# Moving the first feed-forward weight splits to other tiles and other engines at the seam between attention and the first dense layer

## The chip, the core and the metric

The kernel runs on one core of one Trainium2 chip. The metric is the device time of one execution in microseconds (us), as a median over runs. The core has TensorE (PE, with its weight loads shown apart as PEld), VectorE (DVE), ScalarE (ACT), GpSimd (POOL) and SyncE (SP), which here only issues transfers.

## The reference

Three stages follow each other. The first is an attention with pooled queries, the second a dense feed-forward layer, the third a mixture of four dense experts.

```python
q_pool = q.reshape(B, H, S // 2, 2, D).mean(axis=3)          # B 2, H 8, S 1152, D 64
scores = (1 / sqrt(D)) * q_pool @ k.transpose(0, 1, 3, 2)
attn = exp(scores - scores.max(-1)); attn /= attn.sum(-1) + 1e-9
x = (attn @ v) -> rows of 1152 tokens x 512
h = x @ w_in                                                 # 512 -> 2048
x = maximum(0.01 * h, h) @ w_out                             # 2048 -> 512
out = sum_e p[:, e] * (maximum(x @ w1[e], 0) @ w2[e])        # 4 experts, 512 -> 1024 -> 512
```

## The kernel before

Every product is made of three TensorE products: each operand is held as a high half and a low half (`h` and `l`, the rounded value and the rest), and high by high, high by low and low by high are added in PSUM.

**Attention.** It runs over 8 pairs of heads with 9 tiles of 128 query rows each, 72 tiles in all (`tiles`, numbered i; t is the tile within its pair). For a tile, TensorE makes the scores (`emit_s`, line 355), VectorE scales them out of PSUM and takes the row's extreme (line 358), ScalarE makes the exponentials (line 364), VectorE the reciprocal of the sum (line 372), and `emit_norm` multiplies the tile by it (line 374, GpSimd, but VectorE for the last two tiles). TensorE then transposes the tile in three groups of three (line 395) through three PSUM banks, ScalarE copies each group to `th` (line 399) and VectorE makes `tl`, the low half (line 101). The scores run three tiles ahead of the transposes and use the same three PSUM banks each time, so the next scores wait for line 358. The second products (line 422, from `queue_av`) sit in a list, and `run_av` takes a few of them per tile; at the end of each of four column blocks, ScalarE and VectorE write `xf`, `xh` and `xl` (lines 430, 431, 94, 101). These are the layer's input.

**The first dense layer.** It has 16 blocks f of 128 hidden columns. Its weights come as 64-bit numbers whose two 32-bit words need six steps, `split64`, to become two halves of a float: s0 on ScalarE (line 113), s1 and s2 on VectorE (lines 116, 120; with `fast=0` ScalarE's line 122 too), s3 on VectorE, ScalarE and an engine `e` (lines 127, 128, 130), s4 (line 134 on VectorE, or line 136 on GpSimd with `fast=0`), and s5 on `e` (line 139). `e` is VectorE with `fast=2`, and GpSimd otherwise. `prep_a` does this for the input weights (tiles `a`, raw words `wa`), `prep_b` for the output weights (`b`, `wb`). There are three `a` tiles and two raw buffers of each kind; `load_a` and `load_b` issue the next transfer on SP.

For each block TensorE runs 36 products (`first_layer`, lines 190 to 192). The product on line 192 reads the low half of `a`, which the last step, line 139, completes. Then `evac_leaky` has ScalarE take the block out of PSUM (line 589, a leaky relu), write `gh`, and VectorE write `gl`. The first products of block 0 are spread over the last four attention tiles (`f0`). From block 3 on, some 18 or 36 products of the second matrix (`second_moe1`, lines 610 to 612) follow each block.

**What sets the order.** The whole order is written out by hand: the program's order is the queue of each engine, and an engine stops at an instruction whose operands are not ready. `ahead` holds the weight steps that are put between attention tiles; `AT0` says at which tile of the last pair the splits of blocks 0 and 1 begin. Block 2's split (`next_a(2, 2)`) comes after the attention, and so do those of the output weights.

Of the kernel before, what the change touches and what calls it, by code (L numbers as in the profile page):

```python
# [16 lines left out]
ALU = mybir.AluOpType  # L17
# [21 lines left out]
def tile_kernel(ctx: ExitStack, tc: tile.TileContext, q, k, v, w_in, w_out, probs, w1, w2, out):  # L39
# [125 lines left out]
    def prep_a(f, tmp, fast=0):  # L165
        h, l = (a_b[f % 3][:, i] for i in range(2))
        a_t[f] = tuple(t.rearrange("p (a b) -> p a b", a=KD) for t in (h, l))
        return split64(h, l, wa_raw[f % 2].rearrange("p (a b) -> p a b", b=2), tmp, fast)

    def prep_b(f, tmp):  # L170
        h, l = b_t[f] = tuple(b_b[f % 8][:, i] for i in range(2))
        return split64(h, l, wb_raw[f % 2].rearrange("p (a b) -> p a b", b=2), tmp, 1)


    turn = [0]
# [20 lines left out]
    with ExitStack() as actx:  # L196
# [133 lines left out]

        L2 = 6

        AT0 = (0, 6)

        F0N = (0, 2, 2, 2)
        s_sb, chunks = {}, {}
# [33 lines left out]
        def emit_norm(i):  # L370
            e, st = s_sb[i]
            DVE.reciprocal(st[:, 3:4], st[:, 2:3])  # L372
            eng = POOL if i < len(tiles) - 2 else DVE
            eng.tensor_scalar(e, e, st[:, 3:4], 1.0, op0=ALU.mult, op1=ALU.mult)  # L374

        def chunk(n, name):
            if (n, name) not in chunks:
# [72 lines left out]
        with tc.manual_schedule():  # L450
# [52 lines left out]

            def begin(f):
                def go():
                    ahead_a[f] = prep_a(f, tmp)
                return go

            def step(f, i):
                return lambda: ahead_a[f][i] and ahead_a[f][i]()  # L510

            for f, t0 in enumerate(AT0):
                ahead.setdefault(t0, []).extend([begin(f), step(f, 0)])
                for d, ks in enumerate([(1, 2), (3,), (4,), (5,)]):
                    ahead.setdefault(t0 + 1 + d, []).extend([step(f, k_) for k_ in ks])

            for t, load in [(4, load_b), (4, load_b), (AT0[0] + 5, load_a), (AT0[1] + 5, load_a)]:
                ahead.setdefault(t, []).append(load)


# [2 lines left out]
            for i, (n, t) in enumerate(tiles):  # L523
                if i in begin_at:
                    for d, fs in enumerate(prep_pair(begin_at[i])):
                        steps.setdefault(i + d, []).extend(fs)
                lead = 2 if i < L2 else 3

                upto("s", emit_s, i + lead - (i == L2))
                if i == 0:  # L530

                    upto("norm", emit_norm, i + lead - 1)
                upto("sum", emit_sum, i + lead - 1 - (i == L2))
                emit_t(i, lambda: upto("norm", emit_norm, i + lead - 1 - (i == L2)))
                run_av(AVB.get(t, AVD) if i > L2 else AV0.get(t, AVD))
                if i == L2:
                    upto("exp", emit_exp, i + lead - 1)
                    upto("s", emit_s, i + lead)
                    upto("sum", emit_sum, i + lead - 1)
                    upto("norm", emit_norm, i + lead - 1)  # L540
                    run_av(AVD)
                if i == len(tiles) - 4:

                    f0_ps, mms = first_layer(0, xh, xl)
                    f0 = [(k_, c) for k_ in range(KD - 1) for c in range(NC)] + [(KD - 1, c) for c in range(NC)]
                if i >= len(tiles) - 4:
                    for _ in range(F0N[t - 5]):
                        mms(*f0.pop(0))
                upto("exp", emit_exp, i + lead)
                if t in (1, 4, 6, 8):  # L550
                    name, w = {1: ("A1", 256), 4: ("A2", 320), 6: ("B1", 320), 8: ("B2", 256)}[t]
                    queue_av(n, name, w, fast=n == len(pairs) - 1 and t > 4)
                for f in steps.get(i, []):
                    f()
                if n == len(pairs) - 1:
                    for f in ahead.get(t, []):
                        f()
            run_av(1e9)
            for t in range(9, 16):
                for f in ahead.get(t, []):  # L560
                    f()
            while f0:
                mms(*f0.pop(0))

# [7 lines left out]
    def tmp():  # L572
        return next(ring)

    def next_b(f):
        return prep_b(f, tmp) + [load_b]

    def view(t, n=NC):
        return t.rearrange("p (c w) -> p c w", c=n)
# [190 lines left out]

    with tc.manual_schedule():
        SP.dma_start(pr, probs)
        run(next_a(2, 2))
        run(evac_leaky(0, f0_ps), next_a(3), next_b(0))
        ps, mms = first_layer(1, xh, xl)
        for k_ in range(KD):
            for c in range(NC):
                mms(k_, c)
        run(evac_leaky(1, ps), next_b(1))

        when_b = {f: [f - 1] for f in range(3, 15)} | {15: [14, 15]}

# [1 line left out]
        for f in range(2, n1):  # L784
            ps, mms = first_layer(f, xh, xl)
            for k_ in range(KD):
                for c in range(NC):
                    mms(k_, c)
            if f == n1 - 1:
                for b in when_b[f]:  # L790
                    run(next_b(b))
                run(evac_leaky(f, ps))
            else:
                run(evac_leaky(f, ps), next_a(f + 2, f == 2), *[next_b(b) for b in when_b.get(f, [])])
            if f == n1 - 2:
                load_w1(0)
            if f >= GROUPS[second[0][0]][-1] + 2:
                second_moe1(*second.pop(0))
# [88 lines left out]
```

## Time and profile before

| | us |
|---|---|
| median of 3 runs (843.22 to 845.43) | 844.21 |
| the profiled execution | 844.05 |
| its span, from first to last instruction | 842.0 |
| PE busy | 820.8 (97%) |
| VectorE busy | 574.1 (68%) |
| ScalarE busy | 434.5 (52%) |
| GpSimd busy | 417.3 (50%) |

The span is 2.05 us shorter than the execution's time. The attention's last scores end at about 244 us of the span and its last second products at about 261 us; the first dense layer begins at 250.5 us, among the last tiles. The granted clock of TensorE over the span is 0.996 of its full 2.4 GHz.

### The profile page before, as it was taken

The numbers are of one execution on the slowest core, as the hardware profiler recorded it, in microseconds if no ns is written. First come the engines' busy times: TensorE is split into PE (matmuls) and PEld (weight loads), VectorE is DVE, ScalarE is ACT, GpSimd is POOL, SyncE is SP. The second block draws the span as 40 slices with busy tenths as digits, with TensorE's granted clock in tenths as the row PEclk, the third lists the DMA queues.
The fourth block names the chain that finished last, engine by engine and source line by source line (L and its number), as shares of the span: only waits on it lengthen the run. The fifth ranks groups of instructions, "written<-read, shape, count | busy, mean of one in ns | idle before, by whom it ended". The sixth has DMA issues, their size and how long they took to land.

```text
span 842.0 us, 13590 instructions
## 1 busy us (share of the span) xinstructions
PE 820.8 (97%) x5091; PEld 775.6 (92%) x5091; DVE 574.1 (68%) x947; ACT 434.5 (52%) x764; POOL 417.3 (50%) x366
## 2 busy tenths in 40 slices
PE   6899999999989899999999999999999999999998
PEld 5799999999989799999999998989898998989897
DVE  5889999999998979767765762736445363625332
ACT  5889999999976555433432641505142341506030
POOL 3788888888753678556561240506042331504020
PEclk9999999999999999999999999999999999999999
DMA  7347644563401233331130120302011110201012
GB/s 224 90 132 189 181 105 136 162 174 96 138 26 52 100 100 101 100 99 52 51 101 26 51 76 1 100 1 88 13 51 51 50 52 4 98 0 52 0 38 100
DMA packets 25713, 68.65 MB, mean 82 GB/s; under 512 B 2992, under 2 KB 7856, under 8 KB 25648
## 3 DMA queue, kind: packets, MB, share of 16 engines
q1 hardware_dynamic: 25424, 67.43, 26.8%
q8 instruction: 40, 0.66, 0.3%
q10 hardware_dynamic: 224, 0.36, 0.1%
q14 instruction: 25, 0.20, 0.1%
HBM read 48.91 MB, written 2.36 MB: 61 GB/s over the span
## 4 chain that ended last, share of the span: by engine, by line
PE 89%; DVE 7%; issue 2%; ACT 1%; POOL 1%; DMA 1%; SPq 0%; DVEq 0%; POOLq 0%; ACTq 0%
PE ps L713 21%; PE ps L355 9%; PE ps L758 8%; PE ps L760 8%; PE ps L759 8%; PE ps L422 7%; PE ps L395 7%; PE ps L612 4%; PE ps L610 4%; PE ps L611 4%; PE ps L192 3%; PE ps L191 3%; PE ps L190 3%; DVE e L358 2%; DVE tl L101 1%
## 5 line engine op out<-in xcount | busy, mean ns | idle before, releaser
L101 POOL TENSOR_TENSOR bb<-w2r,bb 128x512 fp32r<-128x512 f32 x32 | 40.8, 1297 | 259.0 <-ACT bb L94 259.0
L767 DVE SCALAR_TENSOR_TENSOR oacc<-ps,pw,oacc 128x512 f32<-128x512 f32 (+1 forms) x64 | 47.5, 742 | 100.4 <-PE ps L760 100.4
L101 DVE TENSOR_TENSOR tl<-ps,th 128x384 fp32r<-128x384 f32 (+1 forms) x240 | 112.2, 505 | 3.2 <-ACT th L399 2.8
L758 PE MATMUL ps<-bb,gg 128*128 128x512 f32 (+1 forms) x292 | 112.9, 387 | 0.0
L760 PE MATMUL ps<-bb,gg 128*128 128x512 f32 (+1 forms) x292 | 112.8, 386 | 0.0
L759 PE MATMUL ps<-bb,gg 128*128 128x512 f32 (+1 forms) x292 | 112.8, 386 | 0.0
L713 PE MATMUL ps<-yT,ws 128*128 128x288 f32 x768 | 111.3, 296 | 0.0
L374 POOL TENSOR_SCALAR e<-e,st 128x1152 f32<-128x1152 f32 x70 | 86.3, 1234 | 42.8 <-DVE st L372 25.2
L713 PEld LDWEIGHTS ps<-yT,ws 128*128 128x128 f32 x768 | 105.6, 188 | 0.9 <-ACT cb L730 0.3
L358 DVE TENSOR_SCALAR_CACHE_REDUCE e<-ps 128x1152 f32<-128x1152 f32 x72 | 97.5, 1355 | 11.0 <-PE ps L355 9.7
L355 PE MATMUL ps<-k,qst 128*128 128x384 f32 x438 | 94.4, 346 | 7.9 <-DVE e L358 3.8
L399 ACT CAST th<-ps 128x384 fp32r<-128x384 f32 (+1 forms) x240 | 91.4, 459 | 17.9 <-PE ps L395 16.3
L719 ACT COPY ca<-ps 128x576 f32<-128x576 f32 x16 | 10.3, 641 | 167.1 <-PE ps L713 155.3
L364 ACT ACTIVATE e<-e,st 128x1152 f32<-128x1152 f32 x72 | 91.3, 1268 | 4.8 <-DVE e L358 2.8
L395 PE MATMUL ps<-ident,e 128*128 128x128 f32 x648 | 83.9, 275 | 5.1 <-POOL e L374 3.4
L355 PEld LDWEIGHTS ps<-k,qst 128*128 128x128 f32 x438 | 75.6, 190 | 13.0 <-DVE e L358 6.9
L713 PE MATMUL ps<-yB,ws 128*128 128x288 f32 x576 | 84.4, 296 | 0.0
L395 PEld LDWEIGHTS ps<-ident,e 128*128 128x128 f32 x648 | 75.1, 141 | 9.7 <-POOL e L374 5.1
L713 PEld LDWEIGHTS ps<-yB,ws 128*128 128x128 f32 x576 | 79.6, 188 | 0.6
L192 PE MATMUL ps<-xh,a 128*128 128x384 f32 x192 | 65.1, 339 | 2.8 <-POOL a L139 2.8
L190 PE MATMUL ps<-xh,a 128*128 128x384 f32 x192 | 64.8, 338 | 0.7 <-ACT gf L589 0.7
L760 PEld LDWEIGHTS ps<-bb,gg 128*128 128x128 f32 x292 | 54.9, 188 | 11.4 <-DVE gg L739 0.2
(126 smaller groups left out, 1724.9 us busy)
## 6 DMA issues: line engine op xcount, KB each, us to landing
wa<-in_w_in SPq DMA_DIRECT2D x16, 512.0 KB, 3.4
wb<-in_w_out SPq DMA_DIRECT2D x16, 512.0 KB, 4.3
wf<-in_w SPq DMA_DIRECT2D x32, 256.0 KB, 2.8
w2r<-in_w SPq DMA_DIRECT2D x16, 512.0 KB, 3.4
qst<-rq SPq DMA_DIRECT2D x28, 288.0 KB, 4.6
rv<-in_v SPq DMA_DIRECT2D x8, 576.0 KB, 6.6
rk<-in_k SPq DMA_DIRECT2D x7, 576.0 KB, 6.0
rq<-in_q SPq DMA_DIRECT2D x7, 576.0 KB, 5.3
```

The source lines that it names most:

```text
L101: eng.tensor_tensor(dst, src, f32(high), op=ALU.subtract)
L190: PE.matmul(ps[:, c, :CW], wh[:, k_], src_h[:, k_, cs], start=k_ == 0, stop=False)
L192: PE.matmul(ps[:, c, :CW], wl[:, k_], src_h[:, k_, cs], start=False, stop=k_ == KD - 1)
L355: PE.matmul(ps[:, c, :CW], x, y, start=m == 0, stop=m == len(mms) - 1)
L358: DVE.tensor_scalar(e, ps[:, :, :CW], -0.5 / float(D) ** 0.5, None, op0=ALU.mult, op1=ALU.min, accum_out=st[:, 0:1])
L364: ACT.activation(e, e, AF.Exp, bias=st[:, 0:1], scale=-1.0, accum_out=st[:, 1:2])
L395: PE.transpose(ps[:, j], e[:, (3 * g + j) * 128:(3 * g + j + 1) * 128], ident)
L399: ACT.copy(h, ps[:, :, s0:s0 + w])
L713: PE.matmul(ps[:, c, :HW], w[wi][:, i, ks], y[:, yi, k, c * HW:(c + 1) * HW], start=bool(first and k == 0 and m == 0), stop=k == 1 and m = ...
L758: PE.matmul(ps, gh[:, ts_], wh, start=f == fs[0], stop=False)
L759: PE.matmul(ps, gh[:, ts_], wl, start=False, stop=False)
L760: PE.matmul(ps, gl[:, ts_], wh, start=False, stop=f == fs[-1])
```

## The change

- The split of block 0's input weights starts three tiles earlier: s0 and s1 go to tiles of the pair before, s2 to tile 0, and s3 to s5 stay where they were. `AT0` now gives a tile of the last pair for every step (-3 is the third tile before it).
- Block 1's split gets `fast=2`: what GpSimd and ScalarE's line 122 did in it is VectorE's.
- Block 2's split moves from behind the attention to its last tiles and among the last second products, also with `fast=2`. The list of second products, before emptied in one go, is now emptied block by block between the steps.
- Block 3's and 4's input weights and the first two blocks of output weights get `fast=2`.
- The last two tiles are normalised by GpSimd, not VectorE.
- A one-element leaky relu on ScalarE stands after the last exponential, so that the table load which stood ahead of the first `evac_leaky` stands there.

```diff
-    def prep_b(f, tmp):
+    def prep_b(f, tmp, fast):
...
-        AT0 = (0, 6)
+        AT0 = ((-3, -2, 0, 2, 3, 4), (6, 7, 7, 8, 9, 9), (8, 10, 10, 11, 11, 11))
...
-            eng = POOL if i < len(tiles) - 2 else DVE
-            eng.tensor_scalar(e, e, st[:, 3:4], 1.0, op0=ALU.mult, op1=ALU.mult)
+            POOL.tensor_scalar(e, e, st[:, 3:4], 1.0, op0=ALU.mult, op1=ALU.mult)
...
-                    ahead_a[f] = prep_a(f, tmp)
+                    ahead_a[f] = prep_a(f, tmp, 2 if f else 0)
...
-            for f, t0 in enumerate(AT0):
-                ahead.setdefault(t0, []).extend([begin(f), step(f, 0)])
-                for d, ks in enumerate([(1, 2), (3,), (4,), (5,)]):
-                    ahead.setdefault(t0 + 1 + d, []).extend([step(f, k_) for k_ in ks])
-
-            for t, load in [(4, load_b), (4, load_b), (AT0[0] + 5, load_a), (AT0[1] + 5, load_a)]:
+            for f, ts in enumerate(AT0):
+                ahead.setdefault(ts[0], []).append(begin(f))
+                for k_, t in enumerate(ts):
+                    ahead.setdefault(t, []).append(step(f, k_))
+
+            for t, load in [(4, load_b), (4, load_b), (5, load_a), (9, load_a), (12, load_a)]:
...
-                if n == len(pairs) - 1:
-                    for f in ahead.get(t, []):
-                        f()
-            run_av(1e9)
-            for t in range(9, 16):
+                for f in ahead.get(i + 9 - len(tiles), []):
+                    f()
+                if i == len(tiles) - 3:
+
+                    ACT.activation(warm, warm, AF.Lrelu, alpha=0.01)
+
+            for t in range(9, 13):
                 for f in ahead.get(t, []):
                     f()
+                while t < 11 and av:
+                    cost, f = av.pop(0)
+                    f()
+                    if not cost:
+                        break
+            assert not av
...
-        run(next_a(2, 2))
-        run(evac_leaky(0, f0_ps), next_a(3), next_b(0))
+        run(evac_leaky(0, f0_ps), next_a(3, 2), next_b(0, 2))
...
-        run(evac_leaky(1, ps), next_b(1))
+        run(evac_leaky(1, ps), next_b(1, 2))
...
-                run(evac_leaky(f, ps), next_a(f + 2, f == 2), *[next_b(b) for b in when_b.get(f, [])])
+                run(evac_leaky(f, ps), next_a(f + 2, 2 * (f == 2)), *[next_b(b) for b in when_b.get(f, [])])
```

TensorE's own instructions stand in the same order in both kernels. What moves stands on the other engines, at three places. In the rows below a name's number is that of its buffer: `ct_118` and `c_120`, `c_121` are the splits' scratch tiles, `wa_114` and `wa_115` the raw words of blocks 0 and 1, `a_92`, `a_93`, `a_94` the halves for blocks 0, 1 and 2 and then again from 3 on.

The first place is VectorE's queue in the last two pairs, around the first steps of block 0's split. Before, s1 and s2 stand together ahead of one tile's line 358:

```order
L101 TENSOR_TENSOR tl_74<-ps,th_71 128x3x128
L372 RECIPROCAL st<-st 128x1
L101 TENSOR_TENSOR tl_74<-ps,th_71 128x3x128 x2
L116 TENSOR_SCALAR ct_118<-ct_118 128x512
L120 SCALAR_TENSOR_TENSOR ct_118<-wa_114,ct_118 128x512
L358 TENSOR_SCALAR e_79,st<-ps 128x1152
```

In the changed kernel s1 stands three tiles earlier, ahead of the line 358 that writes `e_76`:

```order
L430 TENSOR_TENSOR xf<-ps,tmp 64x320
L116 TENSOR_SCALAR ct_118<-ct_118 128x512
L358 TENSOR_SCALAR e_76,st<-ps 128x1152
L368 TENSOR_SCALAR st<-st 128x1
L101 TENSOR_TENSOR tl_73<-ps,th_72 128x3x128
```

and s2 one tile earlier, ahead of the one that writes `e_78`:

```order
L101 TENSOR_TENSOR tl_74<-ps,th_71 128x3x128 x2
L430 TENSOR_TENSOR xf<-ps,tmp 64x320
L120 SCALAR_TENSOR_TENSOR ct_118<-wa_114,ct_118 128x512
L358 TENSOR_SCALAR e_78,st<-ps 128x1152
L368 TENSOR_SCALAR st<-st 128x1
```

The second place is VectorE's queue at the last two tiles. Before, line 374 stands between a tile's first and its other two line 101:

```order
L101 TENSOR_TENSOR tl_73<-ps,th_71 128x3x128
L372 RECIPROCAL st<-st 128x1
L374 TENSOR_SCALAR e_76<-e_76,st 128x1152
L101 TENSOR_TENSOR tl_73<-ps,th_71 128x3x128 x2
L368 TENSOR_SCALAR st<-st 128x1
```

In the changed kernel it is gone from there; and a little further on, among the last second products, VectorE's queue holds the end of block 1's split and the start of block 2's around the two last column blocks of the layer's input:

```order
L101 TENSOR_TENSOR tl_74<-ps,th_72 128x3x128 x3
L127 TENSOR_SCALAR wa_115<-ct_119 128x512
L130 TENSOR_TENSOR a_93<-ct_119,a_93 128x512
L134 SCALAR_TENSOR_TENSOR wa_115<-wa_115 128x512
L139 TENSOR_TENSOR a_93<-a_93,wa_115 128x512
L430 TENSOR_TENSOR xf<-ps,tmp 64x320
L101 TENSOR_TENSOR xl<-xf,xh 64x320
L116 TENSOR_SCALAR ct_118<-ct_118 128x512
L120 SCALAR_TENSOR_TENSOR ct_118<-wa_114,ct_118 128x512
L430 TENSOR_TENSOR xf<-ps,tmp 64x256
L101 TENSOR_TENSOR xl<-xf,xh 64x256
```

Before, only line 127 of block 1 stood ahead of these two column blocks, and nothing between them.

The third place is VectorE's queue behind block 0 of the dense layer. Before, it made block 3's `a_92` and the first output weights together with GpSimd, which did their lines 130, 136 and 139:

```order
L101 TENSOR_TENSOR g_103<-gf,g_103 128x1152
L127 TENSOR_SCALAR wa_115<-c_121 128x512
L127 TENSOR_SCALAR wb_116<-c_120 128x512
L134 SCALAR_TENSOR_TENSOR wb_116<-wb_116 128x512
L116 TENSOR_SCALAR c_121<-c_121 128x512
```

In the changed kernel VectorE has all of it, and GpSimd's queue has nothing from the `xl` of the last pair's second column block to block 5's input weights:

```order
L101 TENSOR_TENSOR g_103<-gf,g_103 128x1152
L127 TENSOR_SCALAR wa_115<-c_120 128x512
L130 TENSOR_TENSOR a_92<-c_120,a_92 128x512
L127 TENSOR_SCALAR wb_116<-c_121 128x512
L130 TENSOR_TENSOR b_95<-c_121,b_95 128x512
L134 SCALAR_TENSOR_TENSOR wa_115<-wa_115 128x512
L134 SCALAR_TENSOR_TENSOR wb_116<-wb_116 128x512
L139 TENSOR_TENSOR a_92<-a_92,wa_115 128x512
L139 TENSOR_TENSOR b_95<-b_95,wb_116 128x512
```

## Rows read from the trace of the kernel before

**Rows 1.** Busy time by stretch: length, then busy us (instructions) by engine, granted clock, DMA.

```profile
223.00:250.00 27.00, 24.47 (x176) 22.85 (x175) 26.35 (x65) 22.64 (x50) 16.91 (x18) 1.00 0.09 32
276.00:294.00 18.00, 14.53 (x73) 13.58 (x72) 17.86 (x17) 10.11 (x13) 11.32 (x8) 0.91 0.33 117
290.00:293.40 3.40, 3.31 (x10) 3.32 (x11) 3.40 (x5) 2.60 (x4) 1.73 (x2) 0.50 0.40 154
294.00:480.00 186.00, 186.00 (x1103) 185.83 (x1102) 135.43 (x144) 79.22 (x111) 102.35 (x74) 1.00 0.22 74
```

**Rows 2.** Timeline of TensorE: start, duration, what, and in brackets its idle time before.

```profile
236.21 1.31 PE L355 MATMUL ps<-k,qst 128*128 128x384 f32 x6 [0.64 <-DVE e L358]
240.04 1.31 PE L355 MATMUL ps<-k,qst 128*128 128x384 f32 x6 [0.34 <-DVE e L358]
...
248.52 1.01 PE L395 MATMUL ps<-ident,e 128*128 128x128 f32 x6 [1.24 <-DVE tl L101]
...
254.81 1.14 PE L395 MATMUL ps<-ident,e 128*128 128x128 f32 x9
...
263.20 0.33 PE L190 MATMUL ps<-xh,a 128*128 128x384 f32 x1
...
276.20 0.33 PE L190 MATMUL ps<-xh,a 128*128 128x384 f32 x1
...
277.70 0.44 PE L192 MATMUL ps<-xh,a 128*128 128x384 f32 x1 [0.99 <-POOL a L139]
...
287.68 0.44 PE L190 MATMUL ps<-xh,a 128*128 128x384 f32 x1 [0.68 <-ACT gf L589]
...
290.08 0.69 PE L192 MATMUL ps<-xh,a 128*128 128x384 f32 x1 [1.80 <-POOL a L139]
...
293.44 0.34 PE L190 MATMUL ps<-xh,a 128*128 128x384 f32 x1
```

**Rows 3.** Timeline of VectorE in the last tiles of the attention.

```profile
233.27 0.88 DVE L116 TENSOR_SCALAR ct<-ct 128x512 int32<-128x512 int32 x1
...
246.73 1.27 DVE L374 TENSOR_SCALAR e<-e,st 128x1152 f32<-128x1152 f32 x1
```

**Rows 4.** Timeline of GpSimd at the end of the attention.

```profile
254.60 0.56 POOL L96 TENSOR_SCALAR xh<-xf 64x320 fp32r<-64x320 f32 x1 [7.21 <-DVE xf L431]
```

**Rows 5.** Timeline of VectorE around block 2's split, all of it on VectorE.

```profile
255.85 1.49 DVE L101 TENSOR_TENSOR tl<-ps,th 128x384 fp32r<-128x384 f32 x3 [0.16 <-ACT th L399]
...
261.72 0.43 DVE L431 TENSOR_TENSOR xf<-ps,tmp 64x256 f32<-64x256 f32 x1
262.62 0.42 DVE L101 TENSOR_TENSOR xl<-xf,xh 64x256 fp32r<-64x256 f32 x1 [0.47 <-ACT xh L94]
263.82 0.43 DVE L116 TENSOR_SCALAR c<-c 128x512 int32<-128x512 int32 x1 [0.78 <-ACT c L113]
264.29 0.69 DVE L120 SCALAR_TENSOR_TENSOR c<-wa,c 128x512 int32<-128x512 int32 x1
265.01 0.43 DVE L127 TENSOR_SCALAR wa<-c 128x512 int32<-128x512 int32 x1
...
267.05 0.69 DVE L139 TENSOR_TENSOR a<-a,wa 128x512 fp32r<-128x512 f32 x1
```

**Rows 6.** Timeline of VectorE while GpSimd works on the same splits.

```profile
276.43 1.50 DVE L116 TENSOR_SCALAR c<-c 128x512 int32<-128x512 int32 x1
...
279.56 1.35 DVE L101 TENSOR_TENSOR g<-gf,g 128x1152 fp32r<-128x1152 f32 x1
```

**Rows 7.** Timeline of GpSimd in the same stretch.

```profile
276.04 1.61 POOL L139 TENSOR_TENSOR a<-a,wa 128x512 fp32r<-128x512 f32 x1
```

**Rows 8.** Timeline of ScalarE from the last exponential to block 0's evacuation.

```profile
252.12 1.24 ACT L399 CAST th<-ps 128x384 fp32r<-128x384 f32 x3 [1.48 <-PE ps L395]
...
265.71 1.28 ACT L589 ACT_TABLE_LOAD   x1
267.00 1.14 ACT L589 ACTIVATE gf<-ps 128x1152 f32<-128x1152 f32 x1
```

More of the change, by code (lines that the diff above doesn't have):

```diff
@@ L168, in prep_a @@
         return split64(h, l, wa_raw[f % 2].rearrange("p (a b) -> p a b", b=2), tmp, fast)
-    def prep_b(f, tmp):
+    def prep_b(f, tmp, fast):
         h, l = b_t[f] = tuple(b_b[f % 8][:, i] for i in range(2))
-        return split64(h, l, wb_raw[f % 2].rearrange("p (a b) -> p a b", b=2), tmp, 1)
+        return split64(h, l, wb_raw[f % 2].rearrange("p (a b) -> p a b", b=2), tmp, fast)
     turn = [0]
@@ L573, in tmp, with next_b @@
         return next(ring)
-    def next_b(f):
-        return prep_b(f, tmp) + [load_b]
+    def next_b(f, fast=1):
+        return prep_b(f, tmp, fast) + [load_b]
     def view(t, n=NC):
```

## The prediction, made before the changed kernel was run

> **What bounds the kernel now.** Busy time by stretch comes first. From 294 to 480 us TensorE is busy in all 186.00 us, so there only fewer products would help, and the change takes none away. The two stretches ahead of it are different: TensorE lacks 2.53 us of 27 from 223 to 250, and 3.47 us of 18 from 276 to 294, where its granted clock is 0.91 in the mean and 0.50 from 290.0 to 293.4, which is the 1.2 GHz level [rows 1]. VectorE is busy in 26.35 us of the first of these and in 17.86 of the second [rows 1]: there it is VectorE that limits. So the second view is TensorE's timeline, read for what ended each gap [rows 2].
>
> Up to 276.20 the products follow each other evenly: from 263.20 to 276.20 there are 75, or 0.1733 us each. Then come three gaps: 0.99 us until GpSimd completes block 3's weights (line 139), 0.68 until ScalarE has emptied a PSUM group (line 589), 1.80 until GpSimd completes block 4's weights [rows 2]. Behind the last gap ten products take 3.36 us (290.08 to 293.44) instead of 1.73: the half clock costs 1.62. All together is best read from the ends: from 276.20 to 293.44 there are 36 + 18 + 12 = 66 products, which need 11.44 us and take 17.24. **This seam loses 5.80 us.** It is more than the gaps plus 1.62, since restarts are slow too.
>
> Why are the weights late? A scratch shift (line 116) takes VectorE 0.43 us when GpSimd is still [rows 5], and 1.50 while GpSimd runs a 1.61 us line 139 beside it [rows 6, 7]. Both engines are sharing one job and hold each other up. ScalarE's late line 589 is the same thing at second hand: it waits for VectorE's `gl` of the block before, which stands behind these splits.
>
> In the attention's last pair the gaps are 0.64 and 0.34 us, both until line 358 has read the scores, and 1.24 until line 101 has freed a transposes' bank [rows 2]. Ahead of the first VectorE runs the split of block 0 (a 0.88 us line 116, then line 120) [rows 3]; ahead of the last, the 1.27 us normalisation, line 374 [rows 3].
>
> **The seam, part by part.** Blocks 3 and 4 and the first two output weights go to VectorE alone, and block 2's split is already over by then. For block 3 and the first output weights VectorE has 12 instructions. Alone each takes 0.43 (lines 116, 127) or 0.69 (120 and 139; 130 and 134 are taken as the same) [rows 5]: 4 x 0.43 + 8 x 0.69 = 7.24 us, and the 1.35 us `gl` in their midst [rows 6] makes 8.59. They start behind ScalarE's 1.14 us line 589 [rows 8]: 9.73 us after block 0's end. TensorE wants the low half 72 + 2 products later, after 12.83 us. About 3.1 us are left for ScalarE's casts and the handoffs, so the 0.99 gap goes. The next VectorE round, block 1's `gl` and the second output weights, and then block 4's, are 6 instructions (3.62 us) and a `gl` (1.35) each, 4.97 us in a block that takes TensorE 6.24; VectorE stays ahead, so line 589 is not held and the 0.68 and the 1.80 go. Without these gaps there is no reason for the half clock. I take all of 5.80; the bounds are 0 (a new gap in each place) and 5.80.
>
> What comes after this seam, block 5's weights, is again shared by the two engines, in the same queue order as in all the later rounds, which hold TensorE up nowhere from 294 to 480 [rows 1]. I cost it at nothing; that cover gone is a rival below.
>
> **The last tiles.** Without line 374 between them, VectorE's second and third line 101 start 1.27 us sooner and the gap of 1.24 goes. GpSimd takes both normalisations into a hole of 7.21 us [rows 4]; TensorE wants the first of them two transposes later. Value 1.24, bounds 0 and 1.24. The two steps of block 0's split that now stand apart each meet a tile with a little slack: VectorE has 0.65 us idle in 27 [rows 1], TensorE's own tile is about as long as VectorE's. Line 116 behind a running GpSimd normalisation costs about as now, and one of the two will cost some of it back. Of the two gaps' 0.98 I take three quarters, 0.73; bounds 0 and 0.98. Sum of the last tiles: 1.97.
>
> **What is added on the path.** Block 1's last three steps and block 2's first two now stand ahead of the last two column blocks of the layer's input on VectorE. I set the last transposes' start at 0 (254.81). TensorE reads the last column block's `xl` with its second product behind 263.20, at 8.39 + 0.17 = 8.56 [rows 2]. VectorE's chain: line 101 begins at 1.04 and takes 1.49; lines 127, 130, 134, 139 take 0.43 + 3 x 0.69 = 2.50; a round of `xf`, `xh`, `xl` takes 1.32 (261.72 to 263.04), twice 2.64; lines 116 and 120 between them 1.12 [rows 5]. That makes 8.79, against 8.56: a new wait of 0.2 us. Instructions that don't depend on each other overlap a little (266 to 267 us is such a place), so it may be nothing. I take 0.2, bounds 0 and 1.3 (below). Block 2's weights then end some 2.5 us later, while TensorE needs them a whole block of 6.24 us after block 0.
>
> The table load (1.28 us) leaves the stretch ahead of line 589, where TensorE doesn't wait for it, and goes ahead of the copies of the next-to-last tile. There ScalarE idles 1.48 us for TensorE [rows 8]. Load and a one-element instruction fit; I cost it at nothing.
>
> The Trainium skill (ScalarE: Activation LUTs, section What ACT_TABLE_LOAD costs) speaks against that: it puts a switch of table sets at about 1283 ns for the load and about 1380 ns more for a drain. This trace agrees on the load, and shows line 589 start 0.01 us behind it; ScalarE had nothing running ahead of it to drain [rows 8]. By that page the switch would overrun its hole by some 1.2 us, and the sum below would give 837.7.
>
> **Sum.** 5.80 + 1.97 - 0.20 = 7.57 us less. Against the profiled execution's 844.05 that is 836.48; the profiled one is 0.16 under the median of the runs, so 836.5 stands for the median too.
>
> **The rivals.**
> - *The hole is too short.* If something as long again as the load (1.28) follows it, the copies come 2 x 1.28 - 1.48 = 1.1 us late, VectorE's chain above with them, and the last column block by 1.1 + 0.2: 837.6. For: the chain has no slack. Against: nothing follows the load where it stands now [rows 8]. The same 837 to 839 comes out if the attention's last pair gives back nothing (838.5), because VectorE is full there anyway [rows 1].
> - *The gap moves to block 5.* GpSimd and VectorE then meet with a 1.50 us line 116 again [rows 6], and line 192 of block 5 waits as that of block 4 did, 1.80, with the slow clock's 1.62 behind: 839.9. Against: the later rounds run so without a gap [rows 1].
> - *Slower: VectorE alone is too slow behind block 0.* At the 1.50 us that a slowed instruction takes [rows 6], the 12 would need 18.0, with `gl` and line 589 20.5 us, and block 3's low half would be 7.7 us late; with 1.62 for the clock, 9.3 against the 7.57 saved: 845.8. It decides from a mean of 1.36 us an instruction on. What speaks against it is that GpSimd has nothing to run in that stretch, and that VectorE's durations were 0.43 and 0.69 when it hadn't [rows 5].
>
> **How the numbers follow.** All gaps go, 836.5: 0.64, with 835.0 to 837.8 for its own bounds (no new wait and all of 0.98 at the one end, half of the last tiles' gain and a longer new wait at the other). A short hole, or nothing from the last pair: 0.18. The gap at block 5: 0.10. Slower: 0.05. Something of each kind that leaves less than 2.5 us saved: 0.03. The range 834.7 to 839.2 takes in the first two and the medians' own spread, and leaves out the last three, 0.18. A difference of 0.3%, 2.5 us, is about what a measurement of this kernel can tell from no change; all cases but the last two are beyond it, so faster 0.92, same 0.03, slower 0.05.
>
> **What would show it.** On the seam, the products of blocks 2 to 5 should follow each other at 0.173 us with no gap and a granted clock of 1.00; lines 116 and 127 of blocks 3 and 4 should take 0.43. In the last tiles the 1.24 gap should be gone, and line 374's successor on GpSimd should end well ahead of the transposes. A gap ahead of a line 191 that waits for VectorE's `xl` is the new wait; over 0.5 us, my chain is mis-sized. A gap ahead of line 192 released by VectorE would be the slow rival, one released by GpSimd at block 5 the moved one. Gaps behind 300 us that were not there before would make the prediction wrong in a way that I have not priced.

## The result: 836.71 us, and the profile after

| | before | after |
|---|---|---|
| median, us (runs) | 844.50 (843.22 to 845.43, 4) | 836.71 (836.51 to 836.94, 4) |
| ratio to before (95%) | | 0.9906 (0.9893 to 0.9919) |
| profiled execution / span | 844.05 / 842.0 | 836.74 / 835.0 |
| VectorE busy / GpSimd busy | 574.1 / 417.3 | 569.1 / 403.2 |

The changed kernel is faster by 0.94%, 7.8 us between the medians and 7.31 between the two profiled executions; the prediction had said 7.57.

Busy time by stretch of the changed kernel, with the columns of [rows 1]:

```profile
223.00:250.00 27.00, 26.57 (x190) 24.99 (x189) 25.27 (x65) 24.26 (x51) 20.01 (x20) 1.00 0.09 33
276.00:294.00 18.00, 18.00 (x106) 18.00 (x105) 14.57 (x19) 11.69 (x17) 7.42 (x5) 1.00 0.25 84
294.00:480.00 186.00, 185.88 (x1114) 185.45 (x1113) 137.79 (x145) 80.57 (x113) 103.49 (x74) 1.00 0.24 78
```

The 18 us around the seam are full, at the full clock, and VectorE now has 3.4 us to spare there, where it had 0.14 [rows 1]. TensorE now lacks 0.43 us in the last tiles instead of 2.53. The third row is the only one that got worse, by 0.12.

TensorE's timeline of the changed kernel, against [rows 2]:

```profile
235.91 1.21 PE L355 MATMUL ps<-k,qst 128*128 128x384 f32 x6
...
239.28 1.31 PE L355 MATMUL ps<-k,qst 128*128 128x384 f32 x6
...
246.01 1.44 PE L394 MATMUL ps<-ident,e 128*128 128x128 f32 x9 [0.29 <-DVE st L372]
...
252.76 1.14 PE L394 MATMUL ps<-ident,e 128*128 128x128 f32 x9
...
260.97 0.34 PE L192 MATMUL ps<-xh,a 128*128 128x384 f32 x1
261.31 0.41 PE L190 MATMUL ps<-xh,a 128*128 128x384 f32 x1
261.77 0.41 PE L191 MATMUL ps<-xl,a 128*128 128x384 f32 x1
262.02 0.33 PE L192 MATMUL ps<-xh,a 128*128 128x384 f32 x1
262.19 0.33 PE L190 MATMUL ps<-xh,a 128*128 128x384 f32 x1
...
286.12 0.33 PE L190 MATMUL ps<-xh,a 128*128 128x384 f32 x1
...
330.66 0.34 PE L192 MATMUL ps<-xh,a 128*128 128x384 f32 x1
331.12 0.45 PE L617 MATMUL ps<-g,b 128*128 128x384 f32 x1
331.40 0.34 PE L618 MATMUL ps<-g,b 128*128 128x384 f32 x1
```

The gaps ahead of lines 355 and the 1.24 ahead of the transposes are gone (the 0.29 at 246.01 stood there before too), and the last nine transposes start 2.05 us sooner (254.81 to 252.76). Then come two small losses: from 260.97 to 262.19 four steps take 1.22 us instead of 0.69, and at 331.12 two take 0.74 instead of 0.35. Between them nothing waits: the product that stood at 293.44 is at 286.12, 7.32 sooner. That is 2.05 - 0.53 + 5.80, and 5.80 is what the seam had lost.

VectorE's timeline of the changed kernel, at the last column block, behind block 0, and in a later round:

```profile
261.20 0.42 DVE L101 TENSOR_TENSOR xl<-xf,xh 64x256 fp32r<-64x256 f32 x1 [0.47 <-ACT xh L94]
...
267.56 0.42 DVE L127 TENSOR_SCALAR wa<-c 128x512 int32<-128x512 int32 x1
267.90 0.69 DVE L130 TENSOR_TENSOR a<-c,a 128x512 fp32r<-128x512 f32 x1
...
270.64 0.68 DVE L139 TENSOR_TENSOR a<-a,wa 128x512 fp32r<-128x512 f32 x1
...
320.28 2.61 DVE L116 TENSOR_SCALAR c<-c 128x512 int32<-128x512 int32 x2 [0.32 <-ACT c L113]
...
329.70 1.36 DVE L624 TENSOR_TENSOR yf<-ps,yf 128x1152 f32<-128x1152 f32 x1
```

The last `xl` ends at 261.62, and the product that reads it starts 0.15 later. Block 3's low half is complete at 271.32; TensorE reaches it 72 + 2 products of 0.1733 behind 262.19, at 275.0. The product at 331.12 follows the end of the addition on line 624 (331.06).

ScalarE's timeline of the changed kernel in the last tiles, against [rows 8]:

```profile
247.86 0.68 ACT L113 ACTIVATE ct<-wa 128x512 f32<-128x512 f32 x1
248.56 1.28 ACT L558 ACT_TABLE_LOAD   x1
249.86 0.20 ACT L558 ACTIVATE warm<-warm 128x1 f32<-128x1 f32 x1
250.06 1.24 ACT L398 CAST th<-ps 128x384 fp32r<-128x384 f32 x3
```

The step of a split, the load, the one-element instruction and the copies follow each other without a pause.

### The profile page after: what moved, and what is told of

Read it like the earlier page. It is cut to its first block, busy times and chain, and to the rows that moved or that the text cites. A ratio compares the mean times of both kernels' runs of the same rounds, so it can differ in the third digit from the quotient of the medians.

```text
span 835.0 us, 13582 instructions
## 1 busy us (share of the span) xinstructions
PE 818.8 (98%) x5091; PEld 774.1 (93%) x5091; DVE 569.1 (68%) x957; ACT 433.7 (52%) x763; POOL 403.2 (48%) x356
## 4 chain that ended last, share of the span: by engine, by line
PE 90%; DVE 6%; issue 1%; ACT 1%; DMA 1%; POOL 0%; SPq 0%; DVEq 0%; ACTq 0%
PE ps L720 21%; PE ps L355 9%; PE ps L765 8%; PE ps L767 8%; PE ps L766 8%; PE ps L421 8%; PE ps L394 7%; PE ps L191 4%; PE ps L617 4%; PE ps L190 4%; PE ps L192 4%; PE ps L619 4%; PE ps L618 4%; DVE e L358 2%; DVE tl L101 2%
## 5 line engine op out<-in xcount | busy, mean ns | idle before, releaser
L373 POOL TENSOR_SCALAR e<-e,st 128x1152 f32<-128x1152 f32 x72 | 88.8, 1234 | 41.4 <-DVE st L372 24.0
L767 PEld LDWEIGHTS ps<-bb,gg 128*128 128x128 f32 x292 | 54.8, 188 | 11.4 <-DVE gg L746 0.2
L101 DVE TENSOR_TENSOR ws<-wf,ws 128x768 fp32r<-128x768 f32 (+1 forms) x32 | 44.4, 1386 | 30.1 <-ACT ws L94 30.1
L766 PEld LDWEIGHTS ps<-bb,gg 128*128 128x128 f32 x292 | 54.8, 188 | 10.6
```

What stands on the lines that cost most here:

```text
L101: eng.tensor_tensor(dst, src, f32(high), op=ALU.subtract)
L373: POOL.tensor_scalar(e, e, st[:, 3:4], 1.0, op0=ALU.mult, op1=ALU.mult)
L766: PE.matmul(ps, gh[:, ts_], wl, start=False, stop=False)
L767: PE.matmul(ps, gl[:, ts_], wh, start=False, stop=f == fs[-1])
```

## The experiments

All are edits of the changed kernel, and the line numbers in their rows are a few off from its own. Medians of runs, and the ratio to the kernel before, which was timed beside each group (843.86, 844.32 and 844.33 us):

| kernel | us (range, runs) | ratio (95%) |
|---|---|---|
| norm_vector | 838.30 (838.19 to 838.87, 5) | 0.9932 (0.9918 to 0.9945) |
| steps_together | 837.53 (837.10 to 838.01, 5) | 0.9921 (0.9908 to 0.9935) |
| seam_alone | 838.83 (838.34 to 839.27, 5) | 0.9936 (0.9923 to 0.9948) |
| table_late | 836.92 (836.64 to 837.84, 5) | 0.9917 (0.9901 to 0.9933) |
| short_chain | 836.70 (836.32 to 837.66, 5) | 0.9912 (0.9898 to 0.9926) |
| split_shared | 838.70 (838.35 to 839.09, 5) | 0.9934 (0.9921 to 0.9946) |
| block2_behind | 836.42 (836.18 to 837.03, 4) | 0.9907 (0.9893 to 0.9920) |
| seam_undone | 839.99 (838.73 to 841.23, 5) | 0.9949 (0.9936 to 0.9961) |
| seam_and_table | 840.93 (840.23 to 841.23, 5) | 0.9960 (0.9948 to 0.9973) |
| pool_busy | 845.78 (844.84 to 846.79, 10) | 1.0016 (1.0007 to 1.0025) |
| all_vector | 836.34 (836.04 to 837.07, 4) | 0.9909 (0.9894 to 0.9925) |
| input_vector | 836.48 (836.26 to 837.41, 4) | 0.9910 (0.9897 to 0.9924) |

The changed kernel was not timed again beside these groups, and the profiled executions reach the same transposes early in the kernel between 59.2 and 61.1 us. So a few tenths between medians say little, and the traces are the sharper measure. TensorE does the same products in the same order in every one of these kernels; the next table gives how much longer than in the changed kernel it takes for four stretches of them. A dot stands where the difference is 0.05 us or less, as it is wherever an edit can't reach. The stretches, with their starts and ends in the changed kernel:

- last tiles: from the transposes sixteen tiles before the last (201.21) to the last ones (252.76)
- column block: from there to block 1's first product (262.19)
- seam: from there over 138 products, to block 4's 13th (286.12)
- later round: from there to the 16th product behind the one at 331.12 (334.00)

| us | last tiles | column block | seam | later round |
|---|---|---|---|---|
| kernel before | +2.10 | -0.52 | +5.79 | -0.30 |
| norm_vector | +1.30 | . | . | . |
| steps_together | +0.84 | . | . | . |
| seam_alone | +2.08 | . | . | . |
| table_late | . | . | . | . |
| short_chain | . | -0.52 | . | . |
| split_shared | . | . | +1.30 | +0.50 |
| block2_behind | . | -0.53 | . | . |
| seam_undone | . | -0.53 | +4.06 | -0.25 |
| seam_and_table | . | -0.52 | +3.84 | +0.44 |
| pool_busy | . | . | +7.78 | +0.84 |
| all_vector | . | . | . | -0.39 |
| input_vector | . | . | . | -0.39 |

**The last tiles, one edit at a time and both.** norm_vector:

```diff
-            POOL.tensor_scalar(e, e, st[:, 3:4], 1.0, op0=ALU.mult, op1=ALU.mult)
+            eng = POOL if i < len(tiles) - 2 else DVE
+            eng.tensor_scalar(e, e, st[:, 3:4], 1.0, op0=ALU.mult, op1=ALU.mult)
```

> The changed kernel with only the last two tiles' normalisation back on VectorE. My theory (the normalisation stood ahead of the low halves that free the transposes' banks, and cost TensorE its 1.24 us gap there): the gap of about 1.2 us comes back ahead of the next-to-last transposes, and the time is 836.7 + 1.2 = 837.9. Rival (VectorE is full there anyway, so the gap only moves): no gap of over 0.5 us comes back and the time stays within 0.3 of 836.7.

steps_together:

```diff
-        AT0 = ((-3, -2, 0, 2, 3, 4), (6, 7, 7, 8, 9, 9), (8, 10, 10, 11, 11, 11))
+        AT0 = ((0, 1, 1, 2, 3, 4), (6, 7, 7, 8, 9, 9), (8, 10, 10, 11, 11, 11))
```

> The changed kernel with only the first three steps of block 0's split back at the tiles where the kernel before had them (both VectorE steps ahead of one line 358). My theory (two steps together overrun one tile's slack): gaps ahead of the scores of about 0.6 and 0.3 us come back, less the 0.3 that the parted steps cost, so 836.7 + 0.7 = 837.4. Rival (the steps cost VectorE the same wherever they stand): 836.7, with gaps of the same sum as in the changed kernel.

seam_alone is both of these edits:

> Both edits of the last attention tiles are undone, VectorE normalises the last two tiles and the two steps of block 0's split stand together again; the seam stays changed. Theory A, the two add up as measured one by one: 836.7 + 1.6 + 0.8 = 839.1, with the gaps of 0.64, 0.34 and 1.24 back. Rival B, the second gap swallows part of the first, and what is lost is the 2.05 that the last transposes had gained, less what the shorter wait at the last column block gives: 838.5.

TensorE's timeline of norm_vector (one row), then of steps_together (two rows):

```profile
247.94 1.01 PE L395 MATMUL ps<-ident,e 128*128 128x128 f32 x6 [1.23 <-DVE tl L101]
```

```profile
236.52 1.31 PE L355 MATMUL ps<-k,qst 128*128 128x384 f32 x6 [0.64 <-DVE e L358]
...
240.35 1.31 PE L355 MATMUL ps<-k,qst 128*128 128x384 f32 x6 [0.34 <-DVE e L358]
```

Each edit brings back its own gaps and no other. By the traces they cost 1.30 and 0.84 us one by one and 2.08 together: they add up, as Theory A had it, and the column block's wait doesn't shrink, which Rival B had counted on. The medians give 1.6, 0.8 and 2.1; the 1.6 lies 0.3 above its trace.

**Where the table is loaded.** table_late:

```diff
-                if i == len(tiles) - 3:
-
-                    ACT.activation(warm, warm, AF.Lrelu, alpha=0.01)
```

> The changed kernel without the early leaky relu, so that the table load stands ahead of block 0's evacuation again. My theory (in the changed kernel the weights of blocks 3 and 4 are ready more than 3 us ahead of need, so a load there is hidden as well): block 0's evacuation starts about 0.6 us later, no gap on TensorE, 836.7 within 0.3. Rival 1 (the load stood on the path at the seam): 836.7 + 1.3 = 838.0. Rival 2 (the early load holds up the last column blocks): faster by 0.3 to 0.5.

The ranges of 836.92 and 836.71 overlap, and no stretch of the trace differs: with the rest of the change in place it doesn't matter where the load stands.

**The new wait.** short_chain moves block 1's last step behind one column block and the start of block 2's split behind both:

```diff
-        AT0 = ((-3, -2, 0, 2, 3, 4), (6, 7, 7, 8, 9, 9), (8, 10, 10, 11, 11, 11))
+        AT0 = ((-3, -2, 0, 2, 3, 4), (6, 7, 7, 8, 9, 10), (8, 11, 11, 11, 11, 11))
...
-            for t, load in [(4, load_b), (4, load_b), (5, load_a), (9, load_a), (12, load_a)]:
+            for t, load in [(4, load_b), (4, load_b), (5, load_a), (10, load_a), (12, load_a)]:
```

> The changed kernel with the same work in another order on VectorE at the end of the attention: block 1's last step goes between the last two column blocks (where VectorE waits for ScalarE), block 2's first VectorE steps behind the last one; block 3's transfer moves with it. My theory (the chain of steps ahead of the last column block's low half costs TensorE 0.5 us in the changed kernel): the two waits of 0.16 and 0.29 us at block 0's last three products go, 836.7 - 0.5 = 836.2, and block 2's weights are still ready 2 us early. Rival (what waits there is the second products or ScalarE, not VectorE's queue): the waits stay, 836.7.

The wait is gone, but the median (836.70) doesn't tell it. The profiled execution was the slowest of the five, and lost its time in the first 30 us, where its granted clock was 0.89 against 0.94. So the trace is read from the last transposes to the last product. TensorE's timeline of short_chain, then of the changed kernel:

```profile
254.09 1.14 PE L394 MATMUL ps<-ident,e 128*128 128x128 f32 x9
...
262.31 0.33 PE L192 MATMUL ps<-xh,a 128*128 128x384 f32 x1
...
263.00 0.33 PE L190 MATMUL ps<-xh,a 128*128 128x384 f32 x1
...
832.28 0.28 PE L767 MATMUL ps<-bb,gg 128*128 128x256 f32 x1
```

```profile
831.37 0.28 PE L767 MATMUL ps<-bb,gg 128*128 128x256 f32 x1
```

The four steps that took 1.22 us in the changed kernel (260.97 to 262.19) take 0.69 here (262.31 to 263.00). The whole stretch takes 578.19 us here and 578.61 in the changed kernel: 0.42 less, most of the wait's 0.53.

**The seam's parts.** split_shared gives blocks 3 and 4 and the first output weights back to both engines:

```diff
-        run(evac_leaky(0, f0_ps), next_a(3, 2), next_b(0, 2))
+        run(evac_leaky(0, f0_ps), next_a(3), next_b(0))
...
-        run(evac_leaky(1, ps), next_b(1, 2))
+        run(evac_leaky(1, ps), next_b(1))
...
-                run(evac_leaky(f, ps), next_a(f + 2, 2 * (f == 2)), *[next_b(b) for b in when_b.get(f, [])])
+                run(evac_leaky(f, ps), next_a(f + 2, f == 2), *[next_b(b) for b in when_b.get(f, [])])
```

> The changed kernel with only the engines of blocks 3 and 4 and of the first two output weights as in the kernel before (GpSimd does lines 130, 136, 139); block 2's split stays among the last second products, and the table load early. Theory A, as predicted (the two engines holding each other up cost the 5.8 us): most of it comes back, 840 or more. Theory B (what cost it was the late start: block 2's split and the table load stood ahead of block 0's evacuation; from that evacuation the shared splits need 10.7 us for block 3 and 23 us for block 4, which now come in time or 1.1 us late): no gap at block 3, one of about 1 us at block 4, 837.8, or 839.4 if the clock falls behind it.

block2_behind puts block 2's split behind the attention again:

```diff
-        AT0 = ((-3, -2, 0, 2, 3, 4), (6, 7, 7, 8, 9, 9), (8, 10, 10, 11, 11, 11))
+        AT0 = ((-3, -2, 0, 2, 3, 4), (6, 7, 7, 8, 9, 9))
...
-            for t, load in [(4, load_b), (4, load_b), (5, load_a), (9, load_a), (12, load_a)]:
+            for t, load in [(4, load_b), (4, load_b), (5, load_a), (9, load_a)]:
...
         SP.dma_start(pr, probs)
+        run(next_a(2, 2))
```

> The changed kernel with only block 2's split back behind the attention; the engines stay as changed and the table load early. Theory A (engines): no gap at the seam, and the wait at the last column block goes, 836.2. Theory B (start): block 0's evacuation starts about 1.2 us later; with VectorE alone blocks 3 and 4 are still in time by 2 us, so 836.2 as well. Both are refuted by a time over 837.5. A rival that VectorE is the bound behind block 0: gaps released by VectorE at block 3, 838 or more.

seam_undone is both of these edits:

> The changed kernel with both undone: the engines as before and block 2's split behind the attention; the table load stays early. Theory A (engines): as slow as with the engines alone undone, within 0.5. Theory B (start): clearly slower than with either alone undone, since block 0's evacuation is 1.2 us later than there: gaps of about 2.9 us at the seam, 0.5 back from the last column block, so 839.1, or 840.7 with the slow clock; the rest to the kernel before is then the table load's.

seam_and_table is seam_undone with the edit of table_late:

> As seam_undone, and in addition the one-element leaky relu is taken out, so that the table load stands ahead of block 0's evacuation again. The changed kernel's seam had gained 5.8 us, and seam_undone gave back only 3.3 of it (839.99). Theory A, the load is the rest: ahead of the evacuation its 1.28 us make ScalarE's casts and with them the whole chain of blocks 3 and 4 late; gaps ahead of line 192 of blocks 3 and 4 as before the change, with the half clock behind the second, and 842.3 (the median of before less the 2.05 of the last tiles). Rival B, the load is hidden here too, as it was where only it was undone (836.92): 840.0. Rival C, the load adds its own length and no more: 841.3.

TensorE's gaps in split_shared:

```profile
285.40 0.44 PE L192 MATMUL ps<-xh,a 128*128 128x384 f32 x1 [1.03 <-POOL a L139]
...
332.71 0.45 PE L617 MATMUL ps<-g,b 128*128 128x384 f32 x1 [0.59 <-DVE yf L624]
```

in seam_undone:

```profile
283.61 0.44 PE L190 MATMUL ps<-xh,a 128*128 128x384 f32 x1 [0.22 <-ACT gf L596]
...
286.03 0.66 PE L192 MATMUL ps<-xh,a 128*128 128x384 f32 x1 [1.81 <-POOL a L139]
286.50 0.52 PE L190 MATMUL ps<-xh,a 128*128 128x384 f32 x1
286.81 0.52 PE L191 MATMUL ps<-xl,a 128*128 128x384 f32 x1
```

and in seam_and_table:

```profile
274.72 0.44 PE L192 MATMUL ps<-xh,a 128*128 128x384 f32 x1 [0.51 <-POOL a L139]
...
284.71 0.44 PE L190 MATMUL ps<-xh,a 128*128 128x384 f32 x1 [0.67 <-ACT gf L593]
...
287.12 0.44 PE L192 MATMUL ps<-xh,a 128*128 128x384 f32 x1 [1.79 <-POOL a L139]
287.40 0.33 PE L190 MATMUL ps<-xh,a 128*128 128x384 f32 x1
287.57 0.34 PE L191 MATMUL ps<-xl,a 128*128 128x384 f32 x1
```

Busy time of seam_and_table in that stretch, with the granted clock behind GpSimd's column:

```profile
276.00:294.00 18.00, 15.54 (x88) 14.89 (x87) 17.86 (x17) 10.77 (x14) 11.28 (x9) 1.00 0.32 112
```

Read downwards, the gaps of before come back one after the other. With sharing alone only block 4 waits at the seam, and for 1.03, which is Theory B's trace and not Theory A's 840 or more; undoing block 2's early start alone costs nothing (block2_behind has no gap at the seam). With both undone block 4 waits as long as before, Theory B again; with the table load as well, block 3 and the start of block 4 wait too, and all three gaps of [rows 2] are there. The half clock is not: seam_undone's products behind its 1.81 gap take 0.52 each and stand 0.31 to 0.32 apart, those behind seam_and_table's 1.79 gap take 0.33 and stand 0.17 apart.

**Is sharing the cause, and what would a slow VectorE cost?** pool_busy gives GpSimd ten additions (512 columns each, from two stretches of a `g` tile) behind block 0's splits in the program. Their sums go into a tile that is written anew before anything reads it:

```diff
         run(evac_leaky(0, f0_ps), next_a(3, 2), next_b(0, 2))
+        for _ in range(10):
+            POOL.tensor_tensor(yf[:, 3, :512], f32(g_t[0][0][:, :512]), f32(g_t[0][0][:, 512:1024]), op=ALU.add)
```

> The changed kernel with ten additions of 512 columns on GpSimd behind block 0's high half, which read and write scratch space and are of no use to the result. If the two engines hold each other up: VectorE's lines 116 and 127 go from 0.43 to about 1.5 us while GpSimd runs, block 3's low half ends about 2.7 us after it is needed, with gaps released by VectorE at blocks 3 and 4 and 840 or more. If they do not, and the long instructions of the kernel before came from something else: VectorE's durations stay, 836.7 within 0.4.

VectorE's timeline of pool_busy:

```profile
269.50 1.51 DVE L127 TENSOR_SCALAR wa<-c 128x512 int32<-128x512 int32 x1
270.94 1.77 DVE L130 TENSOR_TENSOR a<-c,a 128x512 fp32r<-128x512 f32 x1
272.63 1.53 DVE L127 TENSOR_SCALAR wb<-c 128x512 int32<-128x512 int32 x1
```

and the gap that it makes on TensorE:

```profile
280.92 0.69 PE L192 MATMUL ps<-xh,a 128*128 128x384 f32 x1 [4.90 <-DVE a L139]
```

With the same instructions on VectorE and only GpSimd made busy, 0.42 becomes 1.51 and 0.69 becomes 1.77; block 3 comes 4.90 us late and 9.1 us are lost. The expectation had 2.7 us, from lines 116 and 127 alone; the lines with two inputs slowed as well.

**The later rounds.** all_vector puts every later split on VectorE as well, input_vector those of the input weights alone:

```diff
-    def next_b(f, fast=1):
+    def next_b(f, fast=2):
...
-                run(evac_leaky(f, ps), next_a(f + 2, 2 * (f == 2)), *[next_b(b) for b in when_b.get(f, [])])
+                run(evac_leaky(f, ps), next_a(f + 2, 2), *[next_b(b) for b in when_b.get(f, [])])
```

> Every split of the first layer's weights from block 3 on is VectorE's alone, the later rounds too. Theory A, sharing is what makes VectorE slow and the late yf addition at 331 us with it: alone the 12 instructions of a round take 7.2 us and gl 1.35, 8.6 in a round of 9.4 (10.0 with the yf addition in a round of 12.5); lines 116 and 127 take 0.43 everywhere, the gap at 331 us goes, 836.3. Rival B, the later rounds live from GpSimd's share: VectorE's queue grows late, gaps ahead of lines 192 or 617 released by VectorE, 838 or more.

(input_vector has the second of these two edits alone.)

> Only the input weights are VectorE's alone in the later rounds, the output weights stay shared with GpSimd. Theory A, contention counts by GpSimd's instructions beside VectorE's: with two of the five left per round, some of VectorE's lines 116 and 127 stay at 1.5 us, and VectorE has 6 instructions of its own and 3 of the shared ones, about 8 to 9 us of 9.4; between the changed kernel and all_vector, 836.5. Rival B, more work on VectorE and the contention with it: VectorE late, 838 or more.

VectorE's line 116 from 294 to 480 us (count, busy us, mean ns of one), of the changed kernel:

```profile
L116 DVE TENSOR_SCALAR c<-c 128x512 int32<-128x512 int32 x21 | 13.2, 638 | 28.0 <-ACT c L113 27.0
```

and of all_vector:

```profile
L116 DVE TENSOR_SCALAR c<-c 128x512 int32<-128x512 int32 x21 | 9.0, 427 | 30.2 <-ACT c L113 28.9
```

with its busy time by engine in the same stretch:

```profile
294.00:480.00 186.00, 186.00 (x1117) 185.89 (x1116) 135.64 (x199) 75.49 (x102) 18.19 (x18) 1.00 0.21 74
```

VectorE does 54 instructions more in 2.15 us less, GpSimd is rid of 85 us, and the gap at 331 is gone, 0.39 us in the trace, in input_vector too. In the medians that is worth nothing that can be told: 836.34 and 836.48 against 836.71, with ranges that overlap. No version beats the changed kernel by more than its spread.

## Why the prediction was right, and where its reasons were not

**The seam, 5.80: the size was right, the reason half right.** The seam runs evenly, as foretold. That GpSimd's work slows VectorE's is shown by pool_busy, which adds such work, and by all_vector, which takes it away. (The reverse no edit tests; in the kernel before GpSimd's line 139 takes 1.61 us there [rows 7] and 1.29 at 246.09.) But the step from two engines that "hold each other up" to gaps that are all due to this failed: with blocks 3 and 4 shared again split_shared keeps all but 2.0 us, of which 1.30 are lost at the seam and 0.50 in the later round, whose wait grows (the step ahead of its line 617 takes 0.92 us instead of 0.46). The early split of block 2 and the load's place, to which the prediction gave no gain at the seam, are indeed worth nothing there one by one. With sharing undone they count: block 2's split another 1.3 us, and the load another 1.3, its own length, which is Rival C of seam_and_table and not its Theory A. These two are read from the seam column, less the half clock in seam_undone: its last ten products there take 3.35 us (286.03 to 289.38), those of seam_and_table 1.87 (287.12 to 288.99). All three give slack to the same chain: the early split or the load's place may go alone for nothing, and sharing alone costs under a quarter of the seam. Block 2's split and the load undone together, with VectorE alone on the splits, was not run. In block2_behind the low halves of blocks 3 and 4 are ready 2.4 and 2.0 us before their products, more than the load's 1.28, so my estimate is that it would cost nothing either.

What is then left of the seam before is 1.95 us: the half clock, 1.49 (3.36 less seam_and_table's 1.87; the prediction's 1.62 goes by an even pace), and the first gap, which is 0.48 longer than in seam_and_table. This 0.48 is sharing once more, at block 1, whose engines no run undoes. VectorE's next-to-last `xl`, before and in seam_and_table:

```profile
260.11 1.51 DVE L101 TENSOR_TENSOR xl<-xf,xh 64x320 fp32r<-64x320 f32 x1 [0.52 <-ACT xh L94]
```

```profile
258.15 0.49 DVE L101 TENSOR_TENSOR xl<-xf,xh 64x320 fp32r<-64x320 f32 x1 [0.52 <-ACT xh L94]
```

Before, GpSimd runs block 1's line 139 beside it (259.96 to 261.27), and block 0's evacuation starts 3.28 us behind block 1's first product; in seam_and_table VectorE has done that split, and it is 2.80. The times fit, but an edit of this alone was not made. In how many of the timed runs the clock fell was not seen: a timed run has only its mean clock.

**The half clock.** "Without these gaps there is no reason for the half clock" held: the seam's granted clock is 1.00. That such a gap always brings it did not. What decides stays open.

**The last tiles, 1.97.** Measured 2.05 from the start of the trace, 2.10 from sixteen tiles before the last. Line 374's share was priced right (1.24; 1.30 when undone), that of block 0's steps a little low (0.73; 0.84). That GpSimd's hole holds both normalisations was right.

**The new wait, 0.20: mis-sized.** It is 0.53, from 260.97 to 262.19. The chain itself was right: `xl` ends 8.86 after the last transposes' start, worked out 8.79. What failed was to set this end against the product's own start, 8.56, as if it could start at once: 0.30 between the two, 0.15 until the product starts behind its `xl` (261.62 to 261.77), and 0.08 because the next one stands 0.25 behind it and not 0.17, make the 0.53. The product before it waits too, for `xh`. The prediction's own line, for a mis-sized chain, had been drawn at 0.5. short_chain shows that the order of block 1's last step and block 2's first ones makes the wait.

**The table load, 0.** Right: it fits its hole, without a gap on TensorE. ScalarE starts the next instruction 0.02 us behind the load though it worked right up to it. The Trainium skill (ScalarE: Activation LUTs, section What ACT_TABLE_LOAD costs) adds a drain of about 1380 ns to every switch of table sets, which would have made 837.7. This trace agrees on the load alone. The prediction had explained the missing drain away: ScalarE "had nothing running ahead of it to drain". That was misread, for ScalarE worked right up to the load (265.71) in the kernel before as well:

```profile
265.07 0.62 ACT L128 CAST a<-c 128x512 fp32r<-128x512 f32 x1 [1.27 <-DVE c L120]
```

**Behind 300 us: one term unpriced.** The gap at 331.12 costs 0.39. That the later rounds "hold TensorE up nowhere" was read from a full stretch, without asking by how little. The same place in the kernel before, on VectorE:

```profile
327.63 2.25 DVE L116 TENSOR_SCALAR c<-c 128x512 int32<-128x512 int32 x2 [0.67 <-ACT c L113]
...
336.70 1.36 DVE L617 TENSOR_TENSOR yf<-ps,yf 128x1152 f32<-128x1152 f32 x1
```

and on TensorE, the product that waits for that addition:

```profile
338.19 0.37 PE L610 MATMUL ps<-g,b 128*128 128x384 f32 x1
```

The addition ended 0.13 ahead of its product; in the changed kernel the product follows it by 0.06. So there was less than 0.1 us of slack. In the changed kernel the two line 116 of that round took 2.61 instead of 2.25, and these 0.36 are nearly all of the gap. With VectorE alone such a pair takes 0.99 to 1.00, and in all_vector there is no gap.

**The sum, 7.57.** 5.80 + 2.05 - 0.53 - 0.39 = 6.93, and the spans differ by 7.0. So the prediction's terms came out 0.64 us lower than it had them. That the profiled executions still differ by 7.31 is due to time outside the span, 2.05 before and 1.74 after, which no term has and no run explains (it is 2.05 to 2.16 in the runs of the kernel before, 1.74 to 1.84 in those of the changed one). To that extent the number's nearness is luck.

**The rivals.** A hole too short: refuted by the profile after. The gap at block 5: refuted, block 5's products follow evenly. A slow VectorE: did not happen. pool_busy, which forces it, gives 845.78 where the rival said 845.8, but that is luck: the rival had block 3 7.7 us late, and it comes 4.90 late, because four of its twelve instructions run before the additions begin; two more gaps at block 4 and the later round's wait make up for it.

## What to carry to other kernels

Before work is split between VectorE and GpSimd, time the same instructions with GpSimd still: here VectorE was busy longer with its half of the work, shared, than with all of it alone. When several edits each give slack to one late chain, undo them together as well as singly, or the parts will seem worth less than the whole. And a stretch without waits shows that it keeps up, not by how much: read the slack at its tightest handoff before you cost what is moved near it at nothing.

## What the runs showed of the hardware

- In pool_busy VectorE's instructions start 1.44 us apart behind a line 127 and 1.69 behind a line 130, where it was 0.34 and 0.60 in the changed kernel: 1.1 more each time, whatever the instruction's length. GpSimd's ten additions there run from 266.67 to 283.68, and in that time VectorE starts ten instructions (267.12 to 282.47): they take turns, one for one. The Trainium skill (SBUF — State Buffer, section Who interferes with whom) says that a VectorE instruction with two inputs in SBUF and a GpSimd instruction that reads SBUF exclude each other, and that the second waits until the first is done; the trace agrees for line 130. The same section counts `tensor_scalar`, with its one tensor input, among those that can contend when they run in a two-port mode. Line 127 is one and waits as long; in which mode it ran no run here shows.
- The granted clock fell behind a gap of 1.80 us before, 1.81 in seam_undone and 4.90 in pool_busy, and did not behind one of 1.79 in seam_and_table or of 1.03 in split_shared. Where it fell, seven to nine products took 0.52 us each instead of 0.33.
- From 294 to 480 us VectorE is busy 137.79 us with 145 instructions when it shares the splits, and 135.64 us with 199 when it does them all.
